# Turning whole q and k units by DMA in a thresholded attention with a two-layer MLP

## The chip, the cores and the metric

The kernel runs on one core of a Trainium2 chip. A core has a matrix engine (TensorE, PE in the profile; its weight loads are PEld), VectorE (DVE), ScalarE (ACT), GpSimd (POOL), and SyncE (SP), which here only issues DMAs. Sixteen DMA engines move data between HBM and the on-chip memory (SBUF), and within SBUF. PE writes to a small memory of its own, PSUM. The metric is the device time of one execution, in microseconds; a version's time is the median of its runs.

## The reference

Per batch and head the scores of 576 queries against 576 keys are thresholded: only keys within tau of the row's maximum take part in the softmax. The result, all heads side by side, goes through a two-layer MLP with a leaky ReLU.

```python
batch, n_heads, seq, head_dim = (8, 8, 576, 64)
scores = scale * np.matmul(q, k.transpose(0, 1, 3, 2))      # scale = 1/8
thresh = np.max(scores, axis=-1, keepdims=True) - tau        # tau = 0.02
scores = np.where(scores >= thresh, scores, -1000000000.0)
attn = softmax(scores)                                       # over the keys
x = (attn @ v), heads side by side: (8 * 576, 512)
h = x @ w_in                                                 # 512 -> 2048
out = np.maximum(0.01 * h, h) @ w_out                        # 2048 -> 512
```

## The kernel before, in words

Heads are worked on in pairs, four pairs a batch. A **step** is one block of 128 queries of one pair against all 576 keys: 16 steps for the first 512 tokens of a batch, and two steps for the last 64 tokens ("tails", two pairs together). That makes 18 steps a batch and 144 in all, numbered n through the whole run. The Python loop at the end of the kernel (L482 to L522) writes the program out step by step; each engine executes its own instructions in that order, and waits on semaphores where it needs another's result. No scheduler moves anything.

**Preparing q and k.** TensorE needs q and k with the head dimension on the partitions, in fp16. For accuracy each value is scaled by 64 and split into a high and a low fp16 half, and the scores are the sum of three products. A **unit** is the q or the k of one pair of heads in one batch: 128 partitions by 512 values, high and low. Ten units a batch: k and q of each of the four pairs, and the tails of k and of q (`units`, L387). For batches 1 to 7 all ten are prepared during the steps of the batch before. Per unit POOL runs `split_scale`, `split_high` and `split_low` (L138, L144, L148), two to three steps ahead; the halves lie in one of four `half` buffers. Then `turn` (L162) transposes: for a whole unit sixteen PE transposes into a PSUM tile `tp` (L177), and one copy of 128x1024 from PSUM to `kT` or `qT`, on ACT (L188). The `tp` tile shares two PSUM buffers (tag `h`) with the MLP's `hp`. A table, `turns_at`, says in which step each unit is turned: counted from the start of the batch that runs meanwhile, at steps 4, 5, 7, 9, 11, 13, 14, 16, 18 and 20 for the units k0, q0, k tails, k1, q1, k2, q2, k3, q3, q tails. Batch 1's are turned closer together, between steps 9 and 22.

**One step.** PE computes the scores of two heads (24 matmuls, `sc`, L217), DVE copies them to SBUF and finds the row's extreme (`s`, L225), POOL adds tau (`th`, L232). Then each head is exponentiated and masked in one of two ways. *Plain*: ACT takes the exponential (`e`, L254), DVE masks it by a comparison, sums the row and writes the weights (`w`, L264). *Steep*: ACT alone does it, with a steep leaky ReLU (L250) that throws masked scores far down and an exponential with the row's sum (L251). Head 0 is always plain; head 1 is steep when `st.steep` is set (L479): in the first twelve steps, and in every step n with no turn at step n + 1. DVE then takes the reciprocal of the sums, POOL writes it, widened, behind the weights (`widen`, L273).

**Turning the weights.** After each second step of a pair (and after each tail step) SP issues one transposing DMA, `wT <- w` (L281): 128 partitions by 2560 values, twenty blocks of 128x128 (ten in a tail step). The first eight steps use PE instead. Four steps after the weights' own step, PE multiplies by v (`pv`, L304, `PV_LAG` = 4), and DVE normalizes (`x`, L326).

**The MLP** is spread over the steps: each step takes one piece of the first layer (`hp`, L347; ACT's leaky ReLU, L349) and two of the second (`o`, L360; ACT's copy, L366).

**SP's queue.** All loads (`raw`, `rawt`, `vraw`, `vrawt`: L79, L88, L93, L100), the stores (L375, L378) and the turns of the weights are issued by SP in the order of the program. Within a step, what stands in `loads_at` comes first, the turn of the weights late, then stores. Loads for the next batch stand at steps -2, 0, 5 and 7 (q and k), 2 and 12 (their tails), 11 and 14 (v) and 13 (v's tails). In the built program each of SP's DMAs waits for the landing of the one issued eight before it, so at most eight are under way.

The functions that the diff touches:

Of the kernel before, what the change touches and what calls it, by code (L numbers as in the profile page):

```python
# [38 lines left out]
def kernel(  # L39
# [10 lines left out]
    nc = tc.nc  # L50
# [3 lines left out]
    MAIN = 512  # L54
# [20 lines left out]
    def load_main(b, s, which, eng=None, parts=1):  # L75
        t = sb.tile([128, 4, 256], FP32, tag="raw", bufs=4, name="raw")
        n = 4 // parts
        for i in range(parts):
            (eng or nc.sync).dma_start(  # L79
                out=t[:, ds(n * i, n), :],  # L80
                in_=SRC[which][b, ds(4 * s + n * i, n), 0:MAIN, :].rearrange("h (p t) d -> p h (t d)", t=4))
        raws[b, s, which] = t

    def load_tails(b, which, eng=None):
        t = sb.tile([128, 2, 2, 64], FP32, tag="rawt", bufs=2, name="rawt")
        src = SRC[which][b, :, MAIN:S, :].rearrange("(u sh) p d -> u p sh d", u=2)
        for u in range(2):
            (eng or nc.sync).dma_start(out=t[ds(64 * u, 64), :, :, :].rearrange("p s h d -> p (s h) d"), in_=src[u])  # L88
        tails[b, which] = t
# [27 lines left out]
    turned, halves, scaled = {}, {}, {}  # L117

    def turned_of(b, which):
        if (b, which) not in turned:  # L120
            turned[b, which] = sb.tile([128, 2, NP, WIDE[which]], FP16, tag=f"{which}T", bufs=2, name=f"{which}T")
        return turned[b, which]
# [7 lines left out]
    def split_scale(key):  # L130
        t = sb.tile([128, 4, 2, 64], FP32, tag="scaled", bufs=2, name="scaled")
        if key[1] == "t":
            src = tails[key[0], key[2]][:, :, :, :]
            dst = t[:, 0:2, :, :]
        else:
            src = pair_of(*key)
            dst = t[:, :, :, :].rearrange("p t h d -> p h t d")
        nc.gpsimd.tensor_scalar(out=dst, in0=src, scalar1=64.0, scalar2=1.0, op0=AX.mult, op1=AX.mult)  # L138
        scaled[key] = t

    def split_high(key):
        n = 2 if key[1] == "t" else 4
        halves[key] = new_half()
        nc.gpsimd.tensor_copy(out=halves[key][:, 0, 0:n, :, :], in_=scaled[key][:, 0:n, :, :])  # L144

    def split_low(key):
        n = 2 if key[1] == "t" else 4
        nc.gpsimd.tensor_tensor(out=halves[key][:, 1, 0:n, :, :], in0=scaled.pop(key)[:, 0:n, :, :],  # L148
                                in1=halves[key][:, 0, 0:n, :, :], op=AX.subtract)
# [12 lines left out]
    def turn(key, copy=None):  # L162
        copy = copy or nc.scalar.copy
        b, p, which = key
        dst, half = turned_of(b, which), halves.pop(key)
        n = 2 if p == "t" else 4
        c0 = 0 if which == "q" else 64
        if p == "t":
            c0 = MAIN if which == "q" else 0
            tp = ps.tile([128, 2, 2, 2, 64], FP16, tag="h", bufs=2, name="tp")  # L170
        else:
            tp = ps.tile([128, 2, 4, 128], FP16, tag="h", bufs=2, name="tp")
        for x in range(2):
            for t in range(n):
                for h in range(2):
                    o = tp[ds(64 * h, 64), x, :, t, :] if p == "t" else tp[ds(64 * h, 64), x, t, :]
                    nc.tensor.transpose(o, half[:, x, t, h, :], ident[:, :])  # L177
        if p == "t":
            for x in range(2):
                copy(out=dst[:, x, :, ds(c0, 64)], in_=tp[:, x, :, :, :].rearrange("d u s p -> d (u s) p"))  # L180
            if which == "k" and b:
                nc.gpsimd.tensor_copy(out=dst[:, :, :, 576:640], in_=dst[:, :, :, 0:64])
            elif which == "k":
                for x in range(2):
                    nc.vector.tensor_copy(out=dst[:, x, :, 576:640],
                                          in_=tp[:, x, :, :, :].rearrange("d u s p -> d (u s) p"))
        else:
            copy(out=dst[:, :, p, ds(c0, 512)], in_=tp[:, :, :, :].rearrange("d x t p -> d x (t p)"))  # L188

# [188 lines left out]


    loads_at, turns_at, pool_at = {}, {}, {}

    def at(d, n, f):
        d.setdefault(n, []).append(f)

    def units(b):  # L387
        u = [(b, p, w_) for p in range(NP) for w_ in "kq"]
        return u[:2] + [(b, "t", "k")] + u[2:] + [(b, "t", "q")]

    for b in range(1, B):
        base = PERB * (b - 1)
        for i, (s, w_) in enumerate(((0, "k"), (0, "q"), (1, "k"), (1, "q"))):
            at(loads_at, base + ((-2, 0, 5, 7)[i] if b > 1 else (3, 4, 8, 9)[i]),
               lambda b=b, s=s, w_=w_: load_main(b, s, w_))
        for i, w_ in enumerate("kq"):
            at(loads_at, base + (2, 12)[i] + 4 * (b == 1), lambda b=b, w_=w_: load_tails(b, w_))
        for i, key in enumerate(units(b)):
            n_ = base + 4 + 18 * i // 10 if b > 1 else 9 + 3 * i // 2
            at(pool_at, n_ - 3, lambda key=key: split_scale(key))  # L400
            at(pool_at, n_ - 3, lambda key=key: split_high(key))
            at(pool_at, n_ - 2, lambda key=key: split_low(key))
            at(turns_at, n_, lambda key=key: turn(key))
    for b in range(B):
        base = PERB * (b - 1)
        if b:
# [52 lines left out]
    for key in first[:3]:  # L459
        split_now(key)  # L460
    turn(first[0])
    turn(first[1], nc.vector.tensor_copy)
    turn(first[2])
    for key in first[3:5]:
# [11 lines left out]

    N = len(steps)
    for st in steps:
        st.steep = st.n < 12 or not turns_at.get(st.n + 1)  # L479
    pv_at = {s.n + PV_LAG - s.early: s for s in steps if s.tail or s.c == 1}  # L480
    n = 0
    while n < N + PV_LAG + 2 or l1q or l2q or stores:  # L482
# [73 lines left out]
```

## Time and profile before

The median of three runs is 521.77 us (521.43 to 523.34). The profiled execution took 523.44 us; its span, from the first to the last instruction, is 521.7 us.

| | busy us | share of the span |
|---|---|---|
| PE | 485.7 | 93% |
| PE weight loads | 342.0 | 66% |
| DVE | 422.7 | 81% |
| ACT | 431.9 | 83% |
| POOL | 331.5 | 64% |
| DMA, SP's queue q1 | | 75.3% of 16 engines' span |

A busy share is an average over the span. "PE" counts matmuls, whose ends are modelled, so a share near 100% says that PE's queue was never empty, not that the array was fully used. The lines quoted below are of these kinds. A line of *groups* has: program line, engine, operation, output <- inputs, shape, count; then busy time and mean ns of one; then the idle time before them and what ended it. A line of the *timeline* has start (us from the span's start), duration, engine, line, operation, tiles, count; SPq is SP's sequencer, and its duration is how long issuing a DMA held SP. A piece of the *chain* (the work that ended last, followed back from the end) has start, duration, and what it was. *Landing* is the time from a DMA's issue to its completion.

### The profile page before, as it was taken

What the parts mean: (1) busy time and instruction counts of PE and PEld (TensorE: products, weight loads), DVE (VectorE), ACT (ScalarE), POOL (GpSimd) and SP (SyncE); (2) the same over time, 40 slices, a digit from 0 to 9 for tenths busy, and PEclk for the clock granted to TensorE, in tenths of its full rate; (3) what the DMA queues carried; (4) which work ended last, traced back from release to release, by engine and by line L of the source; (5) the groups of instructions that cost most, each with busy time, mean ns of one, the idle gap of its engine ahead of it and who ended that gap; (6) DMA issues with size and microseconds to landing.
All of it is one profiled execution on the core that took longest, in us unless ns stands there. A gap on an engine that the chain in (4) does not pass through costs nothing.

```text
span 521.7 us, 19307 instructions
## 1 busy us (share of the span) xinstructions
PE 485.7 (93%) x7904; PEld 342.0 (66%) x7904; DVE 422.7 (81%) x1200; ACT 431.9 (83%) x733; POOL 331.5 (64%) x545
## 2 busy tenths in 40 slices
PE   5777887999999999999999999999999999999996
PEld 3454665667767766677666766667666766667773
DVE  4899998999999878988899888988899888888100
ACT  5699896998988978998889888998889889999541
POOL 4956699787777767677667777687667872222000
PEclk9899899999999999999999999999999999999999
DMA  8992975989968998889979988879969975757611
GB/s 244 249 230 48 175 171 112 177 193 203 230 116 172 200 204 177 168 152 231 191 146 182 194 199 188 163 155 233 186 149 184 195 158 135 127 102 151 134 43 62
DMA packets 220697, 87.76 MB, mean 168 GB/s; under 512 B 190912, under 2 KB 217536, under 8 KB 220608
## 3 DMA queue, kind: packets, MB, share of 16 engines
q1 hardware_dynamic: 217648, 82.07, 75.3%
q0 software_dynamic: 2688, 4.19, 4.4%
q8 instruction: 62, 1.02, 0.8%
q14 instruction: 27, 0.22, 0.1%
q10 hardware_dynamic: 272, 0.26, 0.1%
HBM read 36.70 MB, written 9.44 MB: 88 GB/s over the span
## 4 chain that ended last, share of the span: by engine, by line
PE 65%; DVE 16%; DMA 7%; ACT 6%; POOL 3%; issue 2%; DVEq 0%; POOLq 0%
PE hp L347 20%; PE o L360 18%; PE sc L217 17%; DVE s L225 8%; DMA wT<-w 7%; PE pv L304 6%; DVE w L264 5%; PE tp L177 4%; ACT e L254 1%; ACT s L250 1%; DVE x L326 1%; ACT kT L188 1%; DMA raw<-in_k_dram 1%; POOL half L148 1%; ACT osb L366 1%
## 5 line engine op out<-in xcount | busy, mean ns | idle before, releaser
L225 DVE TENSOR_SCALAR_CACHE_REDUCE s<-sc 128x576 f32<-128x576 f32 x288 | 205.2, 750 | 46.0 <-PE sc L217 40.5
L264 DVE SCALAR_TENSOR_TENSOR w<-s,th,e 128x576 f16<-128x576 f32 x210 | 177.2, 866 | 1.9 <-DMA wT<-w 1.7
L254 ACT ACTIVATE e<-s,mn 128x576 f16<-128x576 f32 x210 | 155.7, 774 | 1.5 <-DVE s L225 1.3
L360 PE MATMUL o<-wout,g 128*64 128x512 f16 x1152 | 147.5, 379 | 0.7 <-ACT osb L366 0.7
L217 PE MATMUL sc<-kT,qT 64*128 64x288 f16 (+1 forms) x1920 | 139.8, 290 | 7.8 <-DVE s L225 7.5
L347 PEld LDWEIGHTS <-win 128*64 128x64 f16 x2560 | 118.4, 110 | 33.0 <-issue 30.7
L347 PE MATMUL hp<-x,win 128*64 128x256 f16 x2048 | 136.8, 277 | 0.0
L349 ACT ACTIVATE g<-hp 128x512 f16<-128x512 f32 x144 | 85.1, 591 | 58.8 <-PE hp L347 58.2
L217 PEld LDWEIGHTS <-qT 64*128 64x128 f16 (+1 forms) x1920 | 78.6, 98 | 61.4 <-issue 46.4
L232 POOL TENSOR_SCALAR th<-mn 128x2 f32<-128x2 f32 x130 | 54.9, 422 | 84.4 <-DVE s L225 56.6
L360 PEld LDWEIGHTS <-g 128*64 128x64 f16 x1152 | 62.1, 110 | 31.3 <-issue 1.5
L148 POOL TENSOR_TENSOR half<-scaled,half 128x512 f16<-128x512 f32 (+1 forms) x75 | 81.5, 1087 | 1.7
L144 POOL CAST half<-scaled 128x512 f16<-128x512 f32 (+1 forms) x75 | 62.5, 834 | 4.8 <-POOL th L232 0.2
L273 POOL CAST w<-rec 128x256 f16<-128x256 f32 (+1 forms) x84 | 32.0, 381 | 52.2 <-DVE rec L270 50.0
L304 PE MATMUL pv<-wT,v 128*64 128x256 f16 (+1 forms) x960 | 54.1, 248 | 9.8 <-DMA wT<-w 5.2
L250 ACT ACTIVATE s<-s,th 128x576 f32<-128x576 f32 x78 | 60.3, 773 | 3.4 <-POOL th L232 1.9
L251 ACT ACTIVATE w<-s,minus_tau 128x576 f16<-128x576 f32 x78 | 60.5, 775 | 2.8
L304 PEld LDWEIGHTS <-v 128*64 128x64 f16 x960 | 40.8, 111 | 29.9 <-DMA wT<-w 11.5
L177 PE MATMUL tp<-ident,half 128*64 128x128 f16 x1152 | 49.3, 229 | 7.6 <-ACT half L158 5.2
L138 POOL TENSOR_SCALAR scaled<-raw 128x512 f32<-128x512 f32 x60 | 48.3, 805 | 7.8 <-DMA raw<-in_k_dram 5.9
L177 PEld LDWEIGHTS <-half 128*64 128x64 f16 x1152 | 42.3, 116 | 11.8 <-ACT half L158 5.9
L188 ACT COPY kT<-tp 128x1024 f16<-128x1024 f16 x32 | 32.3, 1008 | 5.6 <-PE tp L177 5.6
(39 smaller groups left out, 278.8 us busy)
## 6 DMA issues: line engine op xcount, KB each, us to landing
vraw<-in_v_dram SPq DMA_DIRECT2D x16, 512.0 KB, 5.1
out_dram<-osb SPq DMA_DIRECT2D x16, 512.0 KB, 3.4
raw<-in_k_dram SPq DMA_DIRECT2D x14, 512.0 KB, 4.7
raw<-in_q_dram SPq DMA_DIRECT2D x14, 512.0 KB, 4.8
win<-in_moe_w_in_dram POOLq DMA_DIRECT2D x4, 512.0 KB, 10.9
wout<-in_moe_w_out_dram POOLq DMA_DIRECT2D x4, 512.0 KB, 9.1
wT<-w SPq DMA_TRANSPOSE x76, 5.2
raw<-in_k_dram SPq DMA_DIRECT2D x4, 256.0 KB, 4.3
```

Source lines behind the costliest of these rows:

```text
L144: nc.gpsimd.tensor_copy(out=halves[key][:, 0, 0:n, :, :], in_=scaled[key][:, 0:n, :, :])
L148: nc.gpsimd.tensor_tensor(out=halves[key][:, 1, 0:n, :, :], in0=scaled.pop(key)[:, 0:n, :, :], in1=halves[key][:, 0, 0:n, :, :], op=AX.sub ...
L177: nc.tensor.transpose(o, half[:, x, t, h, :], ident[:, :])
L217: nc.tensor.matmul(out=o, lhsT=lhs, rhs=turned[st.b, "k"][rows, kx, pair, ds(key0, 288)], start=(i == 0), stop=(i == 2), skip_group_check= ...
L225: nc.vector.tensor_scalar(out=st.s[:, h, :].rearrange("p (a b) -> p a b", a=2), in0=st.sc[h][:, :, 0:288], scalar1=-1.0 / UNIT, scalar2=No ...
L250: nc.scalar.activation(out=z, in_=z, func=AF.Prelu, bias=st.th[:, h : h + 1], scale=-1.0, alpha=1e20)
L254: nc.scalar.activation(out=st.e[:, h, :], in_=st.s[:, h, :], func=AF.Exp, bias=st.mn[:, h : h + 1], scale=-1.0)
L264: nc.vector.scalar_tensor_tensor(out=st.w[h], in0=st.s[:, h, :], scalar=st.th[:, h : h + 1], in1=st.e[:, h, :], op0=AX.is_le, op1=AX.mult, ...
L304: nc.tensor.matmul(out=o, lhsT=v16[st.b % 2][:, st.p + u, blk, :], rhs=rhs, start=(i == 0), stop=(i == 4), skip_group_check=True)
L347: nc.tensor.matmul(out=hp[ds(64 * u2, 64), jj, :], lhsT=w_in16[:, i, ds(128 * j + 64 * u2, 64)], rhs=g.x[:, i, :], start=(i == 0), stop=(i ...
L349: nc.scalar.activation(out=g.g[:, ds(nj * u, nj), :], in_=hp[:, :, :], func=AF.Prelu, bias=0.0, scale=1.0, alpha=0.01)
L360: nc.tensor.matmul(out=g.o[ds(64 * u2, 64), :], lhsT=g.g[:, j, ds(128 * m + 64 * u2, 64)], rhs=w_out16[:, j, :], start=(j == 0), stop=(j = ...
```

## The change

For batches 1 to 7 the whole units of q and k are no longer transposed by PE and copied by ACT. Two transposing DMAs on SP's queue (one for the high, one for the low half; four blocks of 128x128 each) write them straight from the `half` buffer to `kT` or `qT`. They stand in `loads_at`, at the unit's old step if that is odd, else one step later: steps 5, 5, 9, 11, 13, 15, 17 and 19 for k0, q0, k1, q1, k2, q2, k3, q3. In a step that has loads of q and k they come after those and before loads of v. The tail units keep `turn`, as do all units of batch 0. The choice between steep and plain steps is made by a new set, `plain`: a step is plain when it lies one before the (old) turning step of a k unit or of a tail unit, six steps a batch.

```diff
+    def turn_dma(key):
+        b, p, which = key
+        dst, half = turned_of(b, which), halves.pop(key)
+        for x in range(2):
+            nc.sync.dma_start_transpose(
+                out=dst[:, x, p, ds(0 if which == "q" else 64, MAIN)].rearrange("d (t p) -> d t p", t=4),
+                in_=half[:, x, :, :, :].rearrange("p t h d -> p (t h d)"))
...
     loads_at, turns_at, pool_at = {}, {}, {}
+    plain = set()
...
             at(pool_at, n_ - 2, lambda key=key: split_low(key))
-            at(turns_at, n_, lambda key=key: turn(key))
+            if key[1] != "t":
+
+                at(loads_at, n_ + 1 - n_ % 2, lambda key=key: turn_dma(key))
+            else:
+                at(turns_at, n_, lambda key=key: turn(key))
+            if key[2] == "k" or key[1] == "t":
+                plain.add(n_ - 1)
...
     for st in steps:
-        st.steep = st.n < 12 or not turns_at.get(st.n + 1)
+        st.steep = st.n < 12 or st.n not in plain
```

## The prediction

> **What bounds the kernel now.** I read the page first: busy shares, slices, queues, groups. Three lines carry it.
>
> ```profile
> PE 485.7 (93%) x7904; PEld 342.0 (66%) x7904; DVE 422.7 (81%) x1200; ACT 431.9 (83%) x733; POOL 331.5 (64%) x545
> q1 hardware_dynamic: 217648, 82.07, 75.3%
> PE 65%; DVE 16%; DMA 7%; ACT 6%; POOL 3%; issue 2%; DVEq 0%; POOLq 0%
> ```
>
> TensorE (PE) sets the pace. SP's queue q1 already fills the DMA engines for 75% of the span, and the chain runs through the DMA of wT for 7%. The table of stretches gives DMA shares of 0.83 to 0.92 between 65 and 430 us; after 430, where nothing of a next batch is loaded, 0.67.
>
> Next I read the chain of waits in order of time, in two places: two steps of batch 4, with one turn of a unit, and two steps of batch 7, which turns nothing.
>
> ```profile
> 279.62 0.84 PE sc L217 x12
> 280.46 0.99 PE hp L347 x16
> 281.45 0.45 PE tp L177 x16
> 281.90 0.86 PE o L360 x8
> 282.76 0.55 PE pv L304 x10
> 283.31 0.84 PE sc L217 x12
> ...
> 455.51 0.84 PE sc L217 x12
> 456.35 0.99 PE hp L347 x16
> 457.35 0.86 PE o L360 x8
> 458.21 0.55 PE pv L304 x10
> 458.76 0.84 PE sc L217 x12
> ```
>
> PE goes from one group to the next with no hole. A step with pv takes 283.31 - 279.62 = 3.69 us with the turn and 458.76 - 455.51 = 3.25 without it; the difference is the 0.45 us of sixteen transposes. The pairs around these are 6.4 us and 5.94 us. So PE's transposes lie on the path.
>
> Last I read SP's timeline where the DMAs are thickest, steps 10 to 15 of batch 4 (counted from 251.5 us).
>
> ```profile
> 287.53 3.06 SPq L281 DMA_TRANSPOSE wT<-w  x1
> 290.63 0.59 SPq L375 DMA_DIRECT2D out_dram<-osb  x1
> 291.27 0.44 SPq L93 DMA_DIRECT2D vraw<-in_v_dram  x1
> 291.75 1.58 SPq L88 DMA_DIRECT2D rawt<-in_q_dram  x2
> 293.88 4.57 SPq L281 DMA_TRANSPOSE wT<-w  x1
> 298.49 1.26 SPq L100 DMA_DIRECT2D vrawt<-in_v_dram  x2
> 299.80 1.39 SPq L93 DMA_DIRECT2D vraw<-in_v_dram  x1
> 301.30 3.92 SPq L281 DMA_TRANSPOSE wT<-w  x1
> ```
>
> and, of the same stretch, the chain in order of time:
>
> ```profile
> 301.30 7.46 DMA wT<-w
> 308.80 0.74 PE pv L304 x10
> ```
>
> The first number is the start, the second how long SP is held, or what the chain spends. A turn of one pair's weights (20 blocks of 128x128) holds SP 3.06 us when undisturbed and lands 4.9 us after its issue. The one at 293.88 lands after 8.0 us, the next after 7.5 (the tile's view of 293.5 to 302), and in the chain PE's pv at 308.80 follows at once. Elsewhere there is room: the views by tile give 4.9 to 6.0 us between 274 and 288, where no pv waits for wT. The same late spot returns each batch: landings of 7.8, 7.5, 8.2 and 8.2 us for the issues at 242.1, 301.3, 359.8 and 419.1.
>
> **The change, part by part.**
>
> *PE and ScalarE (ACT).* 7 batches x 8 whole units = 56 units leave PE: 896 of 1152 transposes, 56 x 0.45 = 25 us, on the path nearly everywhere. Their 56 copies out of PSUM (1.008 and 1.006 us in the groups) leave ACT: 56 x 1.007 = 56 us, mostly beside PE's work (the chain has 1% for them). The tails stay.
>
> *Steps masked on both engines.* In the built program 105 steps send their second head to ACT in place of 78. ACT: 27 x (0.773 + 0.775 + 0.187 - 0.774) = +26 us; VectorE (DVE): 27 x (0.866 + 0.080) = -26 us. ACT ends about 30 us lower, DVE 26. Neither ends a PE wait in the steady chain; in batch 7, where every step but one is already of that kind, ACT is at 54.2 of 60 us and PE at 59.8. I cost it at zero. Its cover is PE's 5.94 us a pair; if PE fell below ACT's share of that, ACT would be next.
>
> *SP and the DMA engines.* 112 new transposes of 4 blocks (128 KB each). No row shows that size. From below: the shortest issue of any large transfer on SP, 0.33 us for a store; from above: the shortest 10-block turn, 1.27 us. By blocks, 3.06 / 20 = 0.153 us, so 0.61 us each: it is the same operation, so I take this. A unit is 1.22 us (0.7 to 2.5) on SP and about as long on the DMA engines: the wT at 287.53 is issued in 3.06 us and lands 1.8 us later. Total 68 us in 112 issues, all at odd steps, thus between two turns of wT.
>
> *What is queued behind them.* SP issues in order. At most odd steps the unit fits: SP is free from 3.1 us after one wT issue to the next, 6.2 later. At step 5 a load of raw k (0.57) and two units (2.44) come to 3.0 of 3.1 us; the wT behind them lands some 0.7 us late by the DMA work in front, of which its margin of 1 to 2 us takes most: 0.2 us a batch. In steps 11 to 15 nothing fits: SP's list above has holes of 0.55 and 0.11 us only, and the landing at its end is the one PE waits for. Two units (q of pair 1 ahead of the first late wT, k of pair 2 ahead of the second) go into it: +2.4 us from the issue at 287.53 to pv at 308.80. I give no credit for the 0.55 hole, as the DMA engines are busy through it (a share of 0.87 to 0.95 there).
>
> *Who waits for the units.* The score matmuls, and on POOL the cast that takes the half tile four units later. In steady batches a unit is issued five steps or more (16 us) ahead of its scores, in batch 1 the last one three steps (10 us); behind a wT (3.1 us) with its own 1.2 and some 2 to landing that is 6.3 us. The casts come three steps or more behind. Zero for both, with that slack as the cover; where SP slips by more than 3 us batch 1 pays the rest once.
>
> *The sum.* From one late pv to the next batch's wT of step 10 PE alone sets the time; four units (q of pair 3, both of pair 0, k of pair 1) leave that stretch: 4 x 0.45 = 1.8 us. The other four leave the stretch that SP now sets, where they gain nothing. So a batch changes by -1.8 + 2.4 + 0.2 = +0.8 us, at most 0.1 less for the wT made ready sooner: +0.7. Seven batches: +4.9 us. Batch 0 turns its eight units in 13 steps and not 18; I cost it as one of the seven. The profiled execution took 523.4 us (span 521.7), 0.3% over the median of 521.8, so the forecast is 523.4 + 4.9 = 528.3 for it, and 521.8 + 4.9 = 526.7, or 527, for the median.
>
> [...] The row gives 655 KB / 3.06 us = 214 GB/s. [...]
>
> **The rivals.**
>
> *Faster: the DMAs hide.* For it: a median landing of wT of 5.2 us (the page's list of issues), against 7.5 from issue to pv in the chain above. Against it: the thick spot has no margin. If it holds, PE's 8 x 0.45 = 3.6 us come off seven batches: 25 us, 497. It decides where two units cost the thick spot less than the 1.8 us saved outside it: an issue of 0.45 us (at the lower bound of 0.33 a batch ends at -0.4, the run at 519); between that and full hiding lie 497 to 519.
>
> *Slower: the DMA engines are full everywhere.* The late spot's regime spreads over the batch. The stretches show a share of 0.87 to 0.90 of 59 us; 8 units add 9.8 us, 0.16: 1.04. If the engines can't overlap that, a batch takes 61.4 us: 7 x 2.4 = 17 us, 539. Against it: shares over 1 occur (1.11 at 275 to 281). With the issue at its upper bound of 1.27 us the thick spot alone loses 5.1: 7 x 3.4 = 24 us, 546.
>
> *No change.* Gain and loss are 1.8 and 2.4 us, both rough; 519 to 524.
>
> **How the numbers follow.** A measurement of this kernel tells 0.5% (2.6 us) from no change. Forecast (525 to 533): 0.42. DMAs hide, wholly or in part: 0.32. No change: 0.13. Engines full or dear issues (534 to 550): 0.13. So faster 0.32, same 0.13, slower 0.55. The 80% range leaves out what of the faster case lies below 504 (about 0.1) and the far end of the slow one (under 0.1): 504 to 545. Given the sign of the forecast, its own range is 524.5 to 535.
>
> **What would show it.** Right: DMA_TRANSPOSE kT and qT issues near 0.6 us; q1's share near 88%; ACT's busy time near 400 us and DVE's near 400; PE pv waiting for wT 3 us or more a batch, in steps 13 to 18, in place of 16.7 us in all; pairs of 5.9 to 6.0 us elsewhere. Wrong: issues of 0.4 us or of 1 us; waits for wT spread over all pairs (full engines); the splits on POOL waiting for a half tile still being read by its DMA, which would make the thresholds late, a wait before does not have; or scores waiting for kT or qT, above all at the start of batch 1, whose last unit is turned three steps ahead of its use.

## The result, and the profile after

| | before | after |
|---|---|---|
| median of four runs, us | 522.56 (521.43 to 523.74) | 600.56 (599.73 to 603.51) |
| profiled execution / its span, us | 523.44 / 521.7 | 599.73 / 597.9 |

After takes 1.150 times the time of before (95% interval 1.145 to 1.155): 78 us more, where the prediction had 5 more. (Of the executions below, one of the experiment that moves loads, the profiled one at 616.79 us, and two of the last experiment, 526.07 and 526.57 us, were disturbed: their times are left out, and what that profile shows is not shown for an undisturbed execution.)

The page of after: the engines' busy time, the clock granted to PE in 40 slices (9 is 90% or more), SP's queue q1 (packets, MB, share of 16 engines), and the chain of work that ended last, by engine.

```profile
PE 491.5 (82%) x7008; PEld 327.9 (55%) x7008; DVE 403.2 (67%) x1146; ACT 407.5 (68%) x731; POOL 313.3 (52%) x545
PEclk9889888979999988989799978999999997999999
q1 hardware_dynamic: 278576, 96.76, 81.5%
PE 35%; DMA 29%; DVE 10%; SPq 7%; POOL 7%; ACT 6%; issue 5%; POOLq 0%; DVEq 0%; ACTq 0%
```

PE lost 896 transposes, and yet its busy time is 6 us longer than before's 485.7. Its part of the chain fell from 65% to 35%; the DMAs' part rose from 7% to 29%, and SP's issuing (SPq), which before had none, has 7%. The waits of after (total us, times, longest) say for what PE stops most:

```profile
PE pv L312 <- DMA wT<-w: 77.7, 33, 5.1
```

L312 is pv (L304 before). The line of before is:

```profile
PE pv L304 <- DMA wT<-w: 5.2, 6, 2.4
```

PE's pv waits 77.7 us for turned weights in place of 5.2. The wait grew by 72 us, nearly as much as the time (what else changed on PE is added up further below), and it is for a DMA that the change doesn't touch. What it adds is seen in the lines of `turn_dma`, by line: SP's hold per issue (min/median/max ns), first and last start:

```profile
L194 SPq DMA_TRANSPOSE kT<-half x56: 1188/1267/2773, 35.7 to 506.5; - x56
L194 SPq DMA_TRANSPOSE qT<-half x56: 1196/1266/2649, 54.1 to 513.5; - x56
```

Each new transpose holds SP for 1.27 us, and the fastest of 112 for 1.19; a unit (x2) takes 2.5. SP's timeline of the thick spot of batch 4 (steps 10 to 15, the place that the prediction quoted from before) shows what that does to the queue:

```profile
340.37 2.80 SPq L194 DMA_TRANSPOSE qT<-half  x2
343.21 1.65 SPq L93 DMA_DIRECT2D vraw<-in_v_dram  x1
344.91 1.29 SPq L88 DMA_DIRECT2D rawt<-in_q_dram  x2
346.35 3.79 SPq L289 DMA_TRANSPOSE wT<-w  x1
350.19 2.58 SPq L194 DMA_TRANSPOSE kT<-half  x2
352.82 1.26 SPq L100 DMA_DIRECT2D vrawt<-in_v_dram  x2
354.12 1.55 SPq L93 DMA_DIRECT2D vraw<-in_v_dram  x1
355.84 3.90 SPq L289 DMA_TRANSPOSE wT<-w  x1
359.79 2.58 SPq L194 DMA_TRANSPOSE qT<-half  x2
362.41 0.58 SPq L79 DMA_DIRECT2D raw<-in_k_dram  x1
363.11 4.11 SPq L289 DMA_TRANSPOSE wT<-w  x1
```

and the chain of the same stretch, in order of time:

```profile
346.35 5.37 DMA wT<-w
...
351.77 1.28 PE pv L312 x10
...
355.84 6.00 DMA wT<-w
...
361.88 0.74 PE pv L312 x10
```

SP is never free here: each turn of weights starts the moment the issues ahead of it are done, and the three are 9.5 and 7.3 us apart, where PE's pace needs one every 6. The first two land 5.4 and 6.0 us after their issue, not later than in an easy place before (4.9 to 6.0 us), and pv follows 0.04 us behind. So the weights are late because they were *issued* late.

This is so over the whole batch. From the traces I took, for each turn of weights, the time from the end of POOL's `widen` (the weights are ready) to SP's issue, the time from issue to landing, and PE's idle time right ahead of its pv; means over batches 1 to 6, for the ten turns of a batch (1 to 8 are the pairs' halves, 9 and 10 the tail steps):

| turn | 1 | 2 | 3 | 4 | 5 | 6 | 7 | 8 | 9 | 10 |
|---|---|---|---|---|---|---|---|---|---|---|
| ready to issue, after, us | 0.8 | 0.0 | 5.0 | 2.9 | 0.6 | 3.4 | 7.1 | 4.7 | 9.1 | 4.9 |
| PE idle, after, us | 0.6 | 0 | 3.2 | 0 | 0 | 2.2 | 3.4 | 1.2 | 0.1 | 0.9 |

Before, the first row is 0.0 to 0.2 us in turns 1 to 8 and 0.6 in the ninth. From issue to landing, in turns 1 to 8, before has 5.3 to 7.8 us and after 5.3 to 7.0. PE's idle time at pv grew from 0.9 to 11.6 us a batch.

SP's holds, added up over its timeline between 193 and 429 us: before 72% of the time, 42 us a batch; after 94%, 65 us a batch. Of the rest, in after 4% are gaps under 0.3 us between one issue and the next, and in 2% SP waits; before these are 2% and 26%. With eight units of 2.5 us, SP alone has more to do in a batch than PE, whose busy time is 56 to 59 us. The limit of eight DMAs under way is not what holds SP: of after's 303 issues that have one eight ahead of them, 5 come less than 0.3 us behind its landing (before 1 of 191). The batches, from the first score row of one to that of the next:

| batch | 0 | 1 | 2 | 3 | 4 | 5 | 6 | 7 |
|---|---|---|---|---|---|---|---|---|
| before, us | 60.2 | 60.4 | 59.1 | 58.9 | 58.9 | 59.2 | 59.3 | 52.8 |
| after, us | 64.1 | 78.4 | 69.1 | 70.9 | 68.0 | 70.5 | 70.4 | 53.7 |

Batches 2 to 6 lose 10.7 us each, batch 1 18.1; batch 7, which turns no unit, almost nothing.

### The profile page after: what moved, and what is told of

Read it like the earlier page. It is cut to its first block, busy times and chain, and to the rows that moved or that the text cites. A ratio compares the mean times of both kernels' runs of the same rounds, so it can differ in the third digit from the quotient of the medians.

```text
span 597.9 us, 17630 instructions
## 1 busy us (share of the span) xinstructions
PE 491.5 (82%) x7008; PEld 327.9 (55%) x7008; DVE 403.2 (67%) x1146; ACT 407.5 (68%) x731; POOL 313.3 (52%) x545
## 3 DMA queue, kind: packets, MB, share of 16 engines
q1 hardware_dynamic: 278576, 96.76, 81.5%
## 4 chain that ended last, share of the span: by engine, by line
PE 35%; DMA 29%; DVE 10%; SPq 7%; POOL 7%; ACT 6%; issue 5%; POOLq 0%; DVEq 0%; ACTq 0%
DMA wT<-w 21%; PE hp L355 10%; PE o L368 10%; PE sc L225 10%; DVE s L233 5%; PE pv L312 5%; SPq L194 4%; DMA kT<-half 3%; DVE w L272 3%; DMA rawt<-in_k_dram 2%; POOL half L148 2%; ACT w L259 2%; ACT s L258 1%; POOL scaled L138 1%; POOL half L144 1%
## 5 line engine op out<-in xcount | busy, mean ns | idle before, releaser
L272 DVE SCALAR_TENSOR_TENSOR w<-s,th,e 128x576 f16<-128x576 f32 x183 | 156.9, 873 | 15.9 <-POOL th L240 6.5
L225 PE MATMUL sc<-kT,qT 64*128 64x288 f16 (+1 forms) x1920 | 149.9, 304 | 9.7 <-DVE s L233 8.4
L368 PE MATMUL o<-wout,g 128*64 128x512 f16 x1152 | 150.3, 385 | 0.7 <-ACT osb L374 0.7
L355 PE MATMUL hp<-x,win 128*64 128x256 f16 x2048 | 144.7, 287 | 0.0
L262 ACT ACTIVATE e<-s,mn 128x576 f16<-128x576 f32 x183 | 136.6, 768 | 3.9 <-DVE s L233 3.6
L312 PE MATMUL pv<-wT,v 128*64 128x256 f16 (+1 forms) x960 | 60.8, 266 | 78.8 <-DMA wT<-w 77.7
L312 PEld LDWEIGHTS <-v 128*64 128x64 f16 x960 | 42.5, 117 | 105.8 <-DMA wT<-w 83.0
L259 ACT ACTIVATE w<-s,minus_tau 128x576 f16<-128x576 f32 x105 | 81.4, 775 | 26.1 <-DMA wT<-w 22.8
L258 ACT ACTIVATE s<-s,th 128x576 f32<-128x576 f32 x105 | 80.7, 769 | 25.2 <-POOL th L240 23.0
L138 POOL TENSOR_SCALAR scaled<-raw 128x512 f32<-128x512 f32 x60 | 42.1, 702 | 18.6 <-DMA raw<-in_q_dram 10.7
L374 ACT ACTIVATE osb<-o 128x512 f32<-128x512 f32 x36 | 21.5, 597 | 14.0 <-PE o L368 14.0
L334 DVE TENSOR_TENSOR x<-pv,wT 128x256 f16<-128x256 f32 x64 | 26.9, 420 | 2.3 <-PE pv L312 2.3
L107 POOL CAST v<-vraw 128x256 f16<-128x256 f32 x64 | 24.8, 416 | 0.4
```

Source lines behind the costliest of these rows:

```text
L225: nc.tensor.matmul(out=o, lhsT=lhs, rhs=turned[st.b, "k"][rows, kx, pair, ds(key0, 288)], start=(i == 0), stop=(i == 2), skip_group_check= ...
L258: nc.scalar.activation(out=z, in_=z, func=AF.Prelu, bias=st.th[:, h : h + 1], scale=-1.0, alpha=1e20)
L259: nc.scalar.activation(out=st.w[h], in_=z, func=AF.Exp, bias=minus_tau[:, :], scale=1.0, accum_out=st.sum[h])
L262: nc.scalar.activation(out=st.e[:, h, :], in_=st.s[:, h, :], func=AF.Exp, bias=st.mn[:, h : h + 1], scale=-1.0)
L272: nc.vector.scalar_tensor_tensor(out=st.w[h], in0=st.s[:, h, :], scalar=st.th[:, h : h + 1], in1=st.e[:, h, :], op0=AX.is_le, op1=AX.mult, ...
L312: nc.tensor.matmul(out=o, lhsT=v16[st.b % 2][:, st.p + u, blk, :], rhs=rhs, start=(i == 0), stop=(i == 4), skip_group_check=True)
```

## The experiments

Two explanations stood after these readings. By the one, what costs is the *issue*: a transposing DMA holds SP over a microsecond (1.27 us in the lines above) whatever it carries, and SP works in order. By the other, it is the *bytes*: the DMA engines (q1 81.5% busy) can't carry another 14.7 MB. A second question was where the loss arises: in the thick spot alone, as the prediction had it, or everywhere. Four kernels came first.

**A unit of q in one DMA.** The q main columns get a tile of their own, so that high and low half can be turned in a single DMA of eight blocks; k stays at two. 84 issues in place of 112, the same bytes.

```diff
-        for x in range(2):
-            nc.sync.dma_start_transpose(out=dst[:, x, p, ...], in_=half[:, x, ...])
+        if which == "q":
+            nc.sync.dma_start_transpose(
+                out=qmain_of(b)[:, p, :, :].rearrange("d x (t p) -> d (x t) p", t=4),
+                in_=half[...].rearrange("p x t h d -> p (x t h d)"))
+            return
```

> Each whole q unit of batches 1 to 7 is turned by one DMA of eight blocks, not two of four (its 512 columns lie in a tile of their own); k units keep two. Same bytes, 28 DMAs fewer. Theory 1, SP is held: a small transposing DMA holds SP about 1.27 us whatever its blocks, so a q unit holds it 1.3 and not 2.5 us, 5 us less a batch, seven batches: 600 falls by 35 or more, to 550 to 572, with the wait of wT's issue behind its weights shorter by as much. Theory 2, the DMA engines are full: the bytes are the same, 595 to 605.

Measured: 578.17 us, ratio 1.106 (1.096 to 1.117). The line of the eight-block turn, by line of this kernel:

```profile
L200 SPq DMA_TRANSPOSE qM<-half x28: 1297/1326/3011, 53.1 to 492.4; - x28
```

Twice the blocks, 1.33 us in place of 1.27. The same bytes in fewer issues save 22 us: about 0.8 us for each of the 28 issues that are gone, two thirds of its hold. That is less than the 35 us that the first theory asked for, and more than the second allows.

**A quarter of the bytes.** Batches 2 to 7 turn only the first of four blocks, in as many issues (the turned tile of two batches earlier supplies the rest, so the output is not the reference's).

```diff
+        n = 1 if b > 1 else 4
         for x in range(2):
             nc.sync.dma_start_transpose(
-                out=dst[:, x, p, ds(..., MAIN)].rearrange("d (t p) -> d t p", t=4),
-                in_=half[:, x, :, :, :].rearrange("p t h d -> p (t h d)"))
+                out=dst[:, x, p, ds(..., 128 * n)].rearrange("d (t p) -> d t p", t=n),
+                in_=half[:, x, 0:n, :, :].rearrange("p t h d -> p (t h d)"))
```

> For batches 2 to 7 each of the DMAs turns only the first of its four blocks (the other three quarters of q and k keep older values, so work is left out); batch 1 is whole. Same number of DMAs, a quarter of their bytes. Theory 1, SP is held by each issue: the issue stays near 1.2 us and the time at 590 to 605. Theory 2, the DMA engines are full: three quarters of six batches' new traffic gone, 535 to 555.

Measured: 595.42 us, ratio 1.139 (1.130 to 1.149), 5 us below after. The page's row of q1, and the line of the units (which has batch 1's four-block turns in it):

```profile
q1 hardware_dynamic: 241712, 87.33, 69.0%
```

```profile
L197 SPq DMA_TRANSPOSE kT<-half x56: 1093/1231/2781, 35.7 to 503.0; - x56
L197 SPq DMA_TRANSPOSE qT<-half x56: 1099/1231/2357, 54.1 to 510.0; - x56
```

With q1's share at 69%, below the 75.3% of before, nearly all of the loss is still there, and so is the hold: 1.23 us for 32 KB. This settles the first question: the issues cost, and the bytes that are gone are worth some 5 us of the 78.

**No turn at all.** The same with no DMA for the whole units of batches 2 to 7: what remains is PE and ACT without that work.

```diff
     def turn_dma(key):
         b, p, which = key
         dst, half = turned_of(b, which), halves.pop(key)
+        if b > 1:
+            return
```

> Whole units of batches 2 to 7 are not turned at all (old values of q and k are used, so work is left out); batch 1 is turned by DMA. It shows what the removed work of PE and ACT is worth by itself. If PE's transposes set the pace, as the prediction had it, six batches take 55 us each: 495 to 508. If PE is limited by something else by then, 515 to 522. Theory 1 and 2 agree here.

Measured: 520.49 us, ratio 0.996 (0.993 to 1.000). Batches 2 to 6 take 56.1 to 57.8 us, 1.5 to 2.8 less than before (2.3 in the mean), and batches 0 and 1, which still have batch 1's units by DMA, 9 us more together. Had these two not lost, the run would be at an estimated 511 us, 2% under before: all there was to win from taking this work off PE. The prediction had 3.6 us a batch. The waits of this kernel say where the rest stays:

```profile
PE pv L316 <- DMA wT<-w: 19.9, 15, 3.4
```

With PE faster, late turns of weights hold PE 19.9 us in place of before's 5.2. Half of that lies in batches 0 and 1; in batches 2 to 6 it is 9.4 us, 7.9 of them at turn 7, the thick spot's.

**Loads on another queue.** The loads of q, k and v for batches 2 to 7 are issued by POOL, so that SP has only turns and stores.

```diff
-        nc.sync.dma_start(out=t[:, :, :], in_=v[b, ds(4 * s, 4), ...])
+        (nc.gpsimd if b > 1 else nc.sync).dma_start(out=t[:, :, :], in_=v[b, ds(4 * s, 4), ...])
...
-               lambda b=b, s=s, w_=w_: load_main(b, s, w_))
+               lambda b=b, s=s, w_=w_: load_main(b, s, w_, nc.gpsimd if b > 1 else None))
```

> The loads of q, k and v of batches 2 to 7 are issued by POOL and not by SP; all transposes and stores stay on SP. Same DMAs, same bytes. Theory 1, SP is held: fourteen loads a batch at 0.6 to 0.8 us leave SP, 10 us a batch, six batches: 535 to 555. Theory 2, the DMA engines are full: no change, 595 to 605, or slower by POOL's own issues.

Measured: 603.28 us, one run, no better than after and far from the 535 to 555 of the first theory. SP's timeline suggests why the relief didn't come:

```profile
326.11 5.93 SPq L289 DMA_TRANSPOSE wT<-w  x1
...
348.82 5.96 SPq L289 DMA_TRANSPOSE wT<-w  x1
```

POOL's timeline has a load of raw k issued at 326.03 and one of raw v at 348.74. The two turns of weights issued beside them hold SP 5.9 and 6.0 us in place of 3.4 (the median of after) and land after 9.6 and 12.7 us in place of 5 to 7. Over the batches the mean from issue to landing in four of the ten turns is 9.1 to 10.2 us. What the queue gained, the turns seem to have lost. So this run doesn't tell what a shorter queue alone would bring, and it doesn't agree with the simple form of the theory, by which only SP's total counts.

The next four kernels ask where the loss arises, and look for what is worth keeping.

**The thick spot's two units back on PE** (q of pair 1 and k of pair 2); six by DMA.

```diff
-            if key[1] != "t":
+            if key[1] != "t" and key[1:] not in ((1, "q"), (2, "k")):
```

> Two of the eight units, q of pair 1 (step 11) and k of pair 2 (step 13), are turned on PE again; the other six stay with SP. Theory A, SP is full: what counts is the sum of its holds, 65 us a batch in the changed kernel; two units of 2.8 us go, so a batch falls by 5 to 6 us and the run to 555 to 570. Theory B, the prediction's: only the holds in steps 11 to 15 count, the rest fits into SP's gaps; without those two units the run is at 510 to 525.

Measured: 569.04 us, ratio 1.089 (1.085 to 1.093).

**Only those two by DMA**, the other six on PE, with the old choice of steep steps.

```diff
-            if key[1] != "t":
+            if key[1:] in ((1, "q"), (2, "k")):
...
-        st.steep = st.n < 12 or st.n not in plain
+        st.steep = st.n < 12 or not turns_at.get(st.n + 1)
```

> The opposite: only q of pair 1 and k of pair 2 are turned by SP's DMAs, the other six units on PE, and a step is plain where a turn on PE follows it, as before the change. Theory A: SP is held 42 + 6 = 48 us of 59 a batch, not full, 520 to 532. Theory B: two units of 2.53 us go into the spot that has no margin, 5.1 us a batch less what PE saves, seven batches: 545 to 560.

Measured: 559.27 us, ratio 1.070 (1.065 to 1.076). SP's timeline of the thick spot, where the two turns of weights are 9.0 us apart, and the wait of pv:

```profile
309.34 2.67 SPq L194 DMA_TRANSPOSE qT<-half  x2
...
314.31 3.85 SPq L289 DMA_TRANSPOSE wT<-w  x1
318.19 3.03 SPq L194 DMA_TRANSPOSE kT<-half  x2
...
323.30 4.04 SPq L289 DMA_TRANSPOSE wT<-w  x1
```

```profile
PE pv L312 <- DMA wT<-w: 34.1, 14, 3.8
```

The wait comes 14 times in the run, twice in each of batches 1 to 6 at the turns of the thick spot. Against before (523.08, measured beside it) two units lose 36 us, 2.6 us for each of 14. That this is about the hold of 2.53 is in part chance: pv's wait grew by 29 us (34.1 against 5.2), 2.1 us a unit; 6.3 us of transposes left PE, and PE's clock was halved for longer, 41.5 us against 11.7 (see the last section). The other six lose 46 us, 1.1 us for each of 42. The two losses make 82 us, against the 78 of all eight: they add, about. Theory A has the time of the one kernel, theory B that of the other, and neither has both: both places count, and the six units that "fit" cost more in sum than the two that don't.

The traces say how the two go together. With six units SP is still nearly full: its holds in the whole run fall from after's 480 us to 450, by 30 us, and the span falls by 30 too (25 and 20 in the first experiment). With the thick spot's two units alone they add up to 355 us and SP has time to spare, but not there.

**Two q units in one DMA each** (q of pairs 0 and 3, at steps 5 and 19), the tile of the first experiment, the rest on PE, the old choice of steep steps.

```diff
-            if key[1] != "t":
+            if key[1:] in ((0, "q"), (3, "q")):
```

> Only q of pairs 0 and 3 (steps 5 and 19) are turned by SP, each by one DMA of eight blocks (1.3 us of SP), in places where SP has gaps; all else as before the change. SP is held 45 of 59 us. If the gaps take them, PE saves 2 x 0.45 us a batch: 514 to 518, faster than both kernels. If any hold on SP costs PE, 522 to 528.

Measured: 517.61 us (516.96 to 518.74), against 523.08 (521.15 to 524.82), ratio 0.991 (0.989 to 0.993). Faster than before by 5.5 us, a small gain but outside the spread of both; the sixteen transposes of each of 14 units are 14 x 0.45 = 6.3 us. One thing more differs from before: by the old rule 91 steps are steep and not 78, as no turn on PE follows 13 of them. No run takes this part by itself; in the next experiment 27 such steps make 1.5 us. Its wait of pv:

```profile
PE pv L323 <- DMA wT<-w: 3.7, 6, 1.9
```

The wait for turned weights is no longer than before (5.2), and q1's share, 80.7%, is near after's 81.5 (the slower kernel with the two thick-spot units has 75.6). SP's holds add up to 350 us, those of that kernel to 355: the same load on the queue, and 42 us apart. So while SP is not full the total doesn't decide. Place and number of issues both differ between the two kernels, and no run parts them.

**The old plain steps.** After, with ten plain steps a batch as before.

```diff
-            if key[2] == "k" or key[1] == "t":
-                plain.add(n_ - 1)
+            plain.add(n_ - 1)
```

> The changed kernel with the old choice of plain steps (ten a batch and not six): VectorE masks 26 us more, ScalarE 26 us less. Both theories have neither engine on the path: 595 to 605. If the choice of steps were a cause of the loss, it would fall by more than 10.

Measured: 599.07 us (595.02 and 603.13) against 600.56 for after. The choice of steep steps makes no difference that two runs can show.

The last two kernels ask how much more the gaps take. **k of pair 1 in addition** (two DMAs, step 9), and, in another kernel, **q of pair 2 in addition** (one DMA, step 15):

```diff
-            if key[1:] in ((0, "q"), (3, "q")):
+            if key[1:] in ((0, "q"), (3, "q"), (1, "k")):     # the first
+            if key[1:] in ((0, "q"), (3, "q"), (2, "q")):     # the second
```

> q of pairs 0 and 3 by one DMA each, and k of pair 1 (step 9) by two, with 2.5 us of SP; the rest on PE. Behind step 9 the next weights had 1.7 us of margin in the run with two q units and SP a gap of 3 us. If SP's gaps can be used one by one, PE saves another 0.45 us a batch: 513 to 516. If 2.5 us no longer fit, 518 to 524.

> q of pairs 0, 2 and 3 by one DMA each (steps 5, 15 and 19), the rest on PE. Step 15 lies just behind the crowded spot, where the next weights had 0.7 us of margin, and the unit holds SP 1.3 us. If the hold counts only beyond the margin: 516 to 519, no gain over two units; if SP has caught up by then, 513 to 516.

Measured: 529.84 us, ratio 1.012 (1.008 to 1.016), and 522.17, ratio 0.998 (0.996 to 1.000). Both lie above every range that was given for them. Seven more units in two issues each cost 12 us more than the kernel with two q units, 1.7 us a unit; seven in one issue each 5 us more, 0.7 us a unit. PE's wait for the weights is 17.9 and 9.5 us. Neither of these two places had room for a third unit; others were not tried.

## Why the prediction was wrong

*"PE's transposes lie on the path."* Right as far as it goes: two units in single DMAs gained 5.5 of the 6.3 us that their transposes measure. But of the 3.6 us that eight units are worth a batch, 2.3 came off with no turn at all: PE was busy 3.4 us less a batch and waited 1.2 us more, above all at the thick spot. The rival "the DMAs hide" priced it at 497 us; the kernel without any turn didn't come near.

*"By blocks, 3.06 / 20 = 0.153 us, so 0.61 us each: it is the same operation, so I take this."* This is the step that failed first: an issue took 1.27 us and not 0.61. The hold doesn't scale with the blocks up to ten: in the median it is 1.23 us for one, 1.27 for four, 1.33 for eight and, in before, 1.34 for ten, against 3.36 for twenty. The bound from above, 1.27, was the value. In the kernel that turns one block at a time the least hold is 1.09 us, and a turn lands 3.1 us after its issue in the median. At the median hold SP issues 128 KB (131,072 bytes) of a unit in 1.27 us, which is 103 GB/s, against the 214 that the prediction works out for a long turn.

*"At most odd steps the unit fits: SP is free from 3.1 us after one wT issue to the next, 6.2 later."* The second failure, and the one that makes the prediction's own upper bound (1.27 us an issue, 546 us) too low by 55 us. A gap of 3.1 us takes a unit of 2.5 us only where nothing else stands in it; step 5 has two units and a load, 5.1 + 0.6 us, and stores and the rest of the loads take other gaps. SP's timeline of that step in batch 4 of after, whose weights are ready at 320.57:

```profile
318.75 0.57 SPq L79 DMA_DIRECT2D raw<-in_k_dram  x1
319.37 2.50 SPq L194 DMA_TRANSPOSE kT<-half  x2
321.91 2.57 SPq L194 DMA_TRANSPOSE qT<-half  x2
324.65 3.50 SPq L289 DMA_TRANSPOSE wT<-w  x1
```

What spills over delays the next turn of weights, here by 4.1 us, and with SP held 94% of the time and waiting in 2% it is never made up. The prediction looked at gaps one by one and never added up SP's batch: 42 us and eight times 2.5 are 62 us (65 measured), more than the 55 us PE would have needed; at its own price of 1.22 a unit they would have been 52, and the sum would have shown no harm. The six units that it costed at 0.2 us a batch lose 46 us. Two of its own signs of error came: issues of 1 us and more, and waits for turned weights spread over the batch (at six of the ten turns), though not from the full engines to which it put them.

*The thick spot.* "+2.4 us" for two units of 1.22 was right in kind: nothing there hides a unit. With the measured hold the same sum is 2 x 2.53 = 5.1 us a batch, 35 us a run. The kernel with these two alone lost 36, but that is 29 us of waiting with other terms on top, as said there, and the agreement is partly luck. (The 16.7 us that the prediction gives for pv's wait in before add the waits of PE's weight loads, 11.5, to PE's own 5.2.)

*"Zero for both"* (the scores and POOL's casts waiting for units). The scores wait some 2 us in all. POOL's casts wait 16.9 us (7 times) for a half tile that its DMA still reads. The worst is in batch 1, a wait of 7.5 us at 94 us of the span; the thresholds stand behind it in POOL's order, the third of the prediction's signs of error. Batch 1 is the one that loses 18.1 in place of 10.7 us. Batch 1's own units, costed as the others, are enough for most of the 7.4 more: in the kernel where only they were left to DMA, POOL waited 7.4 us at the same place and batch 1 lost 6.2 us (batch 0 another 2.8).

*Steep and plain.* Costed at zero, measured 1.5 us, inside the spread of the runs (4 to 8 us). ACT's and DVE's busy times, 407.5 and 403.2 us, are as forecast (near 400 each).

*"The DMA engines are full everywhere"* (539 us) was on the right side, but by a mechanism that the run with a quarter of the bytes rules out as the main one. The other half of that rival, dear issues at 1.27 us (546 us), named the right cause, with the loss in the thick spot alone.

So the loss adds up thus. Of the 76.2 us between the two spans, batch 1 has 18.1, batch 0 3.9, batch 7 0.9, and batches 2 to 6 have 10.7 each. In these five PE stands idle for 11.5 us a batch in place of 1.2, nearly all of it ahead of pv: 10.3 us more. It is busy for 58.3 us in place of 57.9, 0.4 us more, though 3.6 us of transposes went; so its other work took 4.0 us longer. PE's clock, below, was halved for 8.3 us a batch there and never before; PE was busy in 7.3 of them, for which an estimated 3.7 us are lost. The clock's part is worked out from the traces; no run isolates it.

## What to carry to other kernels

Price a DMA first by its issue and then by its bytes (here a transposing DMA held SP for 1.23 us with 32 KB and for 1.33 with 256), and take the price of a size that the trace doesn't show from the nearest size that it does show, not by scaling down a much larger one. Before work is moved to an in-order queue, add up all that the queue would have to do in one period and compare it with the period (here 65 us of holds against the 59 that a batch took before); gaps looked at one by one don't show that. A few large DMAs at places with slack are worth something: here two units of eight, in one DMA each, gained 0.9%, and a third, at the two places tried, gave it back or more.

## What the runs showed of the hardware

**A floor under small transposing DMAs.** In the median a turn of 128 KB holds SP for 1.27 us, as long as one of 32 KB (1.23) within 0.04 us, and one of 256 KB (1.33) holds it 0.06 us longer.

**Loads from another queue beside the transposes.** In the kernel whose loads POOL issues, two turns of weights beside such loads landed after 9.6 and 12.7 us, and the slowest of all after 14.6, where after has 7.7 at most. This was seen in one execution and not taken apart; that the loads are the cause is not shown. Units turned from ACT's queue, beside SP's turns, were not tried.

**PE's clock after a stall.** The table of stretches of after (stretch, length, busy time and count for PE, PEld, DVE, ACT and POOL, then the granted clock, DMA share and GB/s) around one stall of PE:

```profile
286.00:288.00 2.00, 2.00 (x32) 1.24 (x24) 1.97 (x8) 1.97 (x5) 0.90 (x3) 1.00 0.60 121
...
290.00:292.00 2.00, 0.00 (x0) 0.00 (x0) 0.00 (x0) 0.12 (x1) 1.32 (x4) 1.00 1.21 271
...
294.00:296.00 2.00, 2.00 (x18) 1.17 (x16) 0.51 (x1) 0.00 (x0) 0.00 (x0) 0.50 0.57 153
```

and the chain behind it, in order of time:

```profile
295.46 1.85 PE hp L355 x16
297.31 1.71 PE o L368 x8
...
299.86 0.99 PE hp L355 x16
300.85 0.86 PE o L368 x8
```

PE stands still for 4.63 us, until the weights land; from 292.1 us on the clock is 0.50 for 6.8 us, hp takes 1.85 us and o 1.71, and after that 0.99 and 0.86 again. After a stall of 1.48 us, at 309.85, hp kept its pace (1.06 us by the timeline before and after it, where the one at 295.39 has 1.92). In the whole span PE is granted half its clock for 73.8 us, mostly in pieces of 3.41 or 6.83 us, against 11.7 us before (41.5 with the two thick-spot units, 11.4 with two q units). PE was busy in 64.1 us of these, before in 9.2; at half the clock the 55 us more are worth an estimated 27 us, and this fits that its busy time rose while its work fell. No one length of stall goes with the halving. From batch 1 to batch 6 of after the clock halves 11 times: 8 times with a stall of 3.4 to 5.1 us, but 3 times with one of only 2.0 to 2.9 us, and one stall of 3.5 us (at 150.3) brings no halving. Behind the stall of 4.63 us, hp and o alone took 1.71 us longer than at their next turn (3.56 against 1.85): there a wait on the path went with a loss beyond its own length.
